# Projecting batch 1's queries with tokens on partitions, and a remainder matmul over all 128 rows

## The chip, the cores and the metric

The kernel runs on one core of one Trainium2 chip. The metric is the time of one execution in microseconds (us), as the device measures it; the median of several runs counts. The profile is one execution recorded by the hardware profiler. TensorE (PE in the profile, its weight loads PEld) multiplies matrices, VectorE (DVE), ScalarE (ACT) and GpSimd (POOL) do elementwise work, and SyncE (SP) issues the transfers.

## The reference

Linear attention followed by a two-layer MLP. For batch b and head h:

```python
def phi(x):
    proj = np.einsum('bhsd,df->bhsf', x, w_phi)
    proj = proj - np.max(np.abs(proj), axis=-1, keepdims=True)
    return np.concatenate([np.exp(proj), np.exp(-proj)], axis=-1)
q_p, k_p = (phi(q), phi(k))
kv = np.einsum('bhsf,bhsd->bhfd', k_p, v)
z = np.sum(k_p, axis=2)
num = np.einsum('bhsf,bhfd->bhsd', q_p, kv)
den = np.einsum('bhsf,bhf->bhs', q_p, z)[..., None] + 1e-06
x = num / den          # 4608 tokens x 512 after the heads are joined
h = x @ w_in           # 512 -> 2048
out = np.maximum(0.01 * h, h) @ w_out   # 2048 -> 512
```

There are 8 batches of 8 heads, 576 tokens and 64 channels; phi has 128 features of each sign. Everything is float32.

## The kernel before, in words

**Precision.** Most products are formed from two rounded parts each. A value x is split into a high part (rounded to the format fp32r) and the remainder, and a product is the sum of high x high, high x low and low x high: three fp32r matmuls. Some attention matmuls of the first batches are plain float32 ones instead; the trace has two records for each.

**Attention** works on pairs of heads; phase number i stands for pair i % 4 of batch i // 4. A k phase projects a pair's keys, exponentiates, and sums features against values into an accumulator (tile `c`); a q phase projects the queries, exponentiates, multiplies with what the k phase left and divides. Batch 0 (i = 0 to 3) has its own functions and runs first. From i = 4 on, `attention()` runs k phase i and q phase i - 1 in turns: both are generators, and each `yield` hands over to the other.

**Two forms of the query projection.** In `q_phase` (L301, all pairs from i = 4) the features stand on partitions and tokens in the free dimension: two matmuls for each of two heads and two half rows of 288 tokens (L319, L320), 32x32 block transposes on VectorE (L321, L340), a maximum over features that needs a reduction (L323) and six small steps across partitions (L325 to L330), a subtraction (L338), the exponentials on ScalarE (L345, L346), the matmuls with the k phase's result (L360), copies of numerator and denominator (L367, L368), and a normalization of all 576 tokens at once (L371 to L376). In `first_q_phase` (L468, batch 0) tokens stand on partitions: three matmuls for 128 tokens and both heads (`proj`, L379), one reduction along the free dimension (L486), one subtraction (L488), transposes on TensorE (L494), exponentials of a whole group of 256 tokens, the matmuls (L516), and a normalization of each group by itself (L523 to L527).

**The last 64 tokens of the keys.** 576 is 4 x 128 + 64. In k phases from i = 8 on, the fifth chunk keeps its 64 tokens in partitions 64 to 127 of the key tile `kst`, and their remainders in partitions 0 to 63 (L269), so that one matmul with `vh` (the same 64 values in both halves) adds high x high and high x low together (L272). The value remainders `vl` of these tokens lie in partitions 64 to 127 alone, and their matmul takes those 64 rows (L271).

**The MoE** takes blocks of 256 tokens (18 blocks). `split` makes the two parts of a block's input x from the ring of attention outputs, head pair by head pair; `layer1` (L568 to L571) accumulates over the four pairs, `layer2` (L588 to L590) follows three steps later. Block 2 is tokens 512 to 767: 64 of batch 0 and the first 192 of batch 1. Block 4 is tokens 1024 to 1279, and is the first with tokens of batch 2. `load_weights` (L146 to L168) rebuilds the weights from two halves of the stored number and splits them, on VectorE and ScalarE; w0 is the first layer's weight and w1 the second's, h and l their parts.

**What sets the order.** A scheduler orders each engine's instructions by priority when the program is built: first batch 0's attention, then the later attention (priority L599), then the weights (L623), then the MoE (L625), each as far as the data that the scheduler expects allow. Each engine then runs its list strictly in order. The accumulators of attention rotate over three buffers of tile `a`.

Of the kernel before, what the change touches and what calls it, by code (L numbers as in the profile page):

```python
# [9 lines left out]
F32 = mybir.dt.float32  # L10
F32R = mybir.dt.float32r
# [33 lines left out]
def attention_moe_kernel(ctx: ExitStack, tc: tile.TileContext, q, k, v, vt, w_phi, w_in, w_out, out):  # L45
# [8 lines left out]
    def st(shape, dt, tag):  # L54
        return sp.tile(shape, dt, tag=tag, name=tag, bufs=BUFS.get(tag, 1))
# [40 lines left out]
    vh = ct([P, 10, 66], F32R, "vh")  # L96
    vl = ct([P, 10, 64], F32R, "vl")
    nc.gpsimd.memset(vh[:, :, 64:66].bitcast(F32), 1.0)

    fr1, fr4 = (cp.tile([P, 2048], F32R, tag="late", name=n, bufs=4) for n in ("fr1", "fr4"))  # L100
    f2, f3 = (cp.tile([P, 2048], F32, tag="late", name=n, bufs=4) for n in ("f2", "f3"))
# [87 lines left out]
    def k_phase(i):  # L189
# [24 lines left out]
        for g in range(3):  # L214
            w = 2 if g < 2 else 1
            r = slice(0, P) if g < 2 else slice(64, P)
            n = P if g < 2 else 64
            m4 = st([P, 4], F32, "m4")
            pmk = st([P, 4, F], F32, "pmk")
            if nat:  # L220
                pk = pt("a")
                for s in range(w):
                    t0 = (2 * g + s) * P if g < 2 else S - P
                    proj(pk, s, kh[:, t0 : t0 + P], kl[:, t0 : t0 + P])
                pkv = pk[r, 0 : 256 * w].rearrange("p (a f) -> p a f", f=F)
            else:
                for s in range(w):
                    t0 = (2 * g + s) * P if g < 2 else S - P
                    pk = pt("a")
                    for j in range(2):  # L230
                        nc.tensor.matmul(pk[:, 256 * j : 256 * j + 256], lhsT=ks[:, j, t0 : t0 + P],
                                         rhs=wq.rearrange("p a f -> p (a f)"), start=True, stop=True)
                    pk = pk[r].rearrange("p (j x f) -> p j x f", j=2, x=2)
                    x = pmk[r, 2 * s : 2 * s + 2]
                    copy_("pk", x, pk[:, :, 1])
                    nc.vector.tensor_tensor(x, pk[:, :, 0], x, op=ALU.add)
                    yield
                pkv = pmk[r, 0 : 2 * w]
            nc.vector.tensor_reduce(m4[r, 0 : 2 * w], pkv, axis=AX.X, op=ALU.max, apply_absolute_value=True)
            mb = m4[r, 0 : 2 * w].unsqueeze(2).broadcast_to([n, 2 * w, F])  # L240
            if nat:
                nc.vector.tensor_tensor(pmk[r, 0 : 2 * w], pkv, mb, op=ALU.subtract)
            else:
                tt_("ksub", pkv, pkv, mb, ALU.subtract)
            yield
            for s in range(w):
                c = 2 * g + s
                ek = st([P, 2, 256], F32, ("ek", "kph", "kpl")[c % 3] if nat else "ek")
                nc.scalar.activation(ek[r, :, 0:F], pmk[r, 2 * s : 2 * s + 2], AF.Exp)  # L249
                nc.scalar.activation(ek[r, :, F:256], pmk[r, 2 * s : 2 * s + 2], AF.Exp, scale=-1.0)  # L250
                if nat:
                    for j in range(2):
                        kv_mm(j, rv[r, 4 * j + c if c < 4 else 8 + j], ek[r, j], first=c == 0, last=c == 4)
                    yield
                    continue
                if c < 4:
                    kph = st([P, 2, 256], F32R, "kph")
                    kpl = st([P, 2, 256], F32R, "kpl")
                    copy_("kph", kph, ek)
                    tt_("kpl", kpl, ek, kph.bitcast(F32), ALU.subtract)  # L260
                    for j in range(2):
                        kv_mm(j, vh[:, 4 * j + c], kph[:, j], first=c == 0)
                        kv_mm(j, vl[:, 4 * j + c], kph[:, j])
                    for j in range(2):
                        kv_mm(j, vh[:, 4 * j + c], kpl[:, j])
                else:
                    kst = st([P, 2, 256], F32R, "kph")
                    copy_("kst", kst[r], ek[r])
                    nc.vector.tensor_tensor(kst[0:64], ek[r], kst[r].bitcast(F32), op=ALU.subtract)  # L269
                    for j in range(2):  # L270
                        kv_mm(j, vl[r, 8 + j], kst[r, j])  # L271
                        kv_mm(j, vh[:, 8 + j], kst[:, j], last=True)  # L272
                yield
        kvs = st([P, 2, 256], F32, "ek").rearrange("p a (b f) -> p a b f", b=2)[0:66]
# [23 lines left out]
    def blocks(x):  # L298
        return x.rearrange("p a b -> p (a b)").rearrange("p (c d) -> p c d", d=32)

    def q_phase(i):  # L301
        b, hp = divmod(i, NP)
        nat = i < NN
        rq = qraw.pop(i)
        qs = st([P, 2, S], F32R, "qs")
        for j in range(2):
# [24 lines left out]
        yield  # L331
        kvh, kvl = kvs_of[i]
        dn = tq[:, 0]
        if not nat:
            qhs = st([P, 2, 2, U], F32R, "qh")
        for j in range(2):
            tj = blocks(tq[:, j])
            nc.vector.tensor_tensor(tj, tj, m[:, j].unsqueeze(2).broadcast_to([P, 18, 32]), op=ALU.subtract)  # L338
# [4 lines left out]
            for u in range(2):  # L343
                eq = st([P, 2, U], F32, "eq")
                nc.scalar.activation(eq[:, 0], mb[:, u], AF.Exp)  # L345
                nc.scalar.activation(eq[:, 1], mb[:, u], AF.Exp, scale=-1.0)  # L346
                if nat:
                    es.append((eq, None))
                else:
                    qh = qhs[:, u]  # L350
                    ql = st([P, 2, U], F32R, "ql")
                    copy_("qh", qh, eq)
                    tt_("ql", ql, eq, qh.bitcast(F32), ALU.subtract)
                    es.append((qh, ql))
                yield
            for u in range(2):
                qh, ql = es[u]
                nm = pt("a")[:, 0:U]
                for t in range(2):
                    nc.tensor.matmul(nm, lhsT=kvh[:, j, t], rhs=qh[:, t], start=t == 0, stop=nat and t == 1)  # L360
                    if not nat:
                        nc.tensor.matmul(nm, lhsT=kvl[:, j, t], rhs=qh[:, t], start=False, stop=False)  # L362
                if not nat:
                    for t in range(2):
                        nc.tensor.matmul(nm, lhsT=kvh[:, j, t], rhs=ql[:, t], start=False, stop=t == 1)  # L365
                rr = slice(64 * j, 64 * j + 64)
                nc.scalar.copy(ring[rr, b % 2, hp, U * u : U * u + U], nm[0:64])  # L367
                nc.scalar.activation(dn[rr, u], nm[64:128], AF.Copy, bias=1e-6)  # L368
                yield
# [5 lines left out]
        x = ring[:, b % 2, hp]  # L375
        tt_("x", x, x, dt.rearrange("p a b -> p (a b)"), ALU.mult)  # L376
        yield

    def proj(pk, s, lh, ll, n=P):  # L379
        o = pk[0:n, 256 * s : 256 * s + 256]  # L380
        nc.tensor.matmul(o, lhsT=lh, rhs=bd_h, start=True, stop=False)
        nc.tensor.matmul(o, lhsT=lh, rhs=bd_l, start=False, stop=False)
        nc.tensor.matmul(o, lhsT=ll, rhs=bd_h, start=False, stop=True)

    def first_kvh(i):
        if i == 0:
# [150 lines left out]
    def attention():  # L537
        for i in range(NP, B * NP + 1):
            gens = [k_phase(i)] if i < B * NP else []
            if i > NP:  # L540
                gens.append(q_phase(i - 1))
            while gens:
                for it in list(gens):
                    if next(it, end) is end:
# [130 lines left out]
```

## Time and profile before

| | |
|---|---|
| three timed runs | 1243.72, 1244.25 and 1248.7 us, median 1244.25 |
| profiled execution, first to last instruction (the only time that the profile gives of it) | 1244.1 us |
| busy share of that span | TensorE 95%, weight loads 84%, VectorE 69%, ScalarE 65%, GpSimd 55% |
| mean granted TensorE clock | 0.986 |
| first matmul of blocks 0, 1, 2 and 4 | 65.9, 174.8, 238.9 and 387.0 us |

In the profile's rows a time is in us from the start of the span unless it is marked as a mean in ns; a group's row ends with the idle time of the engine just before its instructions. A busy time of TensorE counts overlapping matmuls; how much of the engine a matmul takes is seen from one start to the next. A row of windows gives a stretch, its length, the busy time and number of instructions of PE, PEld, DVE, ACT and POOL (those that have any), the granted clock, and the transfers' share and GB/s.

### The profile page before, as it was taken

The page shows a single profiled execution, that of the slowest core. Times are in us where ns is not written, and L with a number is a line of the kernel's source. Part 1 is how long each engine was busy: PE and PEld are TensorE (multiplying, and loading weights), DVE is VectorE, ACT ScalarE, POOL GpSimd, SP SyncE. Part 2 cuts the span into 40 slices and gives each one's busy share as a digit, 9 for nine tenths or more (in the row PEclk, how much of TensorE's full clock was granted, in tenths as well). Part 3 has the DMA queues.
Part 4 walks back from the last instruction along what each step waited for, and adds up shares of the span by engine and source line. Part 5 has one row for each costly group of instructions (what it writes and reads, how often), then busy time and mean ns, then how long its engine had stood idle before and what let it go on. Part 6 is the DMA issues. An engine that isn't in the chain of part 4 may idle for free. (4 is left out here: it accounts for less than half of the span.)

```text
span 1244.1 us, 21315 instructions
## 1 busy us (share of the span) xinstructions
PE 1183.8 (95%) x7554; PEld 1041.1 (84%) x7554; DVE 862.9 (69%) x1373; ACT 806.0 (65%) x2044; POOL 688.4 (55%) x711
## 2 busy tenths in 40 slices
PE   6889889989999999999999999999999999999998
PEld 5577568879888888899888988889988888999997
DVE  7999985688888888888888888816887788200000
ACT  6897766767677777777676777635766767433232
POOL 2132122466777776767667676835666766433232
PEclk9899989979999999999999999999999999999999
DMA  6544511011111111111111111100111100000000
GB/s 190 150 118 145 142 56 42 19 47 30 48 31 39 39 30 48 31 47 31 34 30 42 30 48 30 31 29 27 31 47 31 27 21 1 18 18 1 18 18 17
DMA packets 62777, 57.00 MB, mean 46 GB/s; under 512 B 45136, under 2 KB 46288, under 8 KB 62672
## 3 DMA queue, kind: packets, MB, share of 16 engines
q1 hardware_dynamic: 62672, 55.65, 15.7%
q8 instruction: 59, 0.97, 0.3%
q14 instruction: 46, 0.38, 0.1%
HBM read 46.20 MB, written 9.44 MB: 45 GB/s over the span
## 5 line engine op out<-in xcount | busy, mean ns | idle before, releaser
L72 POOL TENSOR_TENSOR gl<-g,gh 128x256 fp32r<-128x256 f32 x288 | 246.7, 860 | 300.7 <-ACT gh L67 239.9
L568 PE MATMUL h<-xh,w0h 128*128 128x256 f32 x1152 | 297.6, 285 | 6.0 <-ACT w0h L67 3.3
L569 PE MATMUL h<-xh,w0l 128*128 128x256 f32 x1152 | 296.7, 284 | 1.7 <-DVE w0l L72 1.6
L588 PE MATMUL acc<-w1h,gh 128*128 128x512 f32 x576 | 229.4, 399 | 7.7 <-DVE o L69 3.6
L568 PEld LDWEIGHTS h<-xh,w0h 128*128 128x128 f32 x1152 | 219.4, 190 | 18.4 <-ACT w0h L67 3.9
L569 PEld LDWEIGHTS h<-xh,w0l 128*128 128x128 f32 x1152 | 219.7, 191 | 13.6 <-DVE w0l L72 4.1
L589 PE MATMUL acc<-w1l,gh 128*128 128x512 f32 x576 | 227.9, 396 | 0.3 <-DVE w1l L72 0.3
L590 PE MATMUL acc<-w1h,gl 128*128 128x512 f32 x576 | 219.5, 396 | 0.3 <-POOL gl L72 0.3
L571 PE MATMUL h<-xl,w0h 128*128 128x256 f32 x1152 | 207.5, 284 | 0.9 <-POOL rv L179 0.5
L575 ACT ACTIVATE g<-h 128x256 f32<-128x256 f32 x288 | 108.6, 382 | 125.3 <-PE h L571 86.6
L72 POOL TENSOR_TENSOR ql<-eq,qh 128x576 fp32r<-128x576 f32 x96 | 158.1, 1657 | 34.3 <-DVE qh L69 23.6
L571 PEld LDWEIGHTS h<-xl,w0h 128*128 128x128 f32 x1152 | 167.9, 190 | 3.8 <-POOL rv L179 0.8
L67 ACT CAST gh<-g 128x256 fp32r<-128x256 f32 x288 | 115.0, 403 | 78.8 <-PE acc L589 77.5
L72 POOL TENSOR_TENSOR kpl<-ek,kph 128x512 fp32r<-128x512 f32 x72 | 103.4, 1436 | 50.3 <-PE c L211 26.9
L588 PEld LDWEIGHTS acc<-w1h,gh 128*128 128x128 f32 x576 | 108.4, 188 | 23.1 <-DVE o L69 4.8
L590 PEld LDWEIGHTS acc<-w1h,gl 128*128 128x128 f32 x576 | 106.5, 189 | 18.9 <-POOL gl L72 0.5
L589 PEld LDWEIGHTS acc<-w1l,gh 128*128 128x128 f32 x576 | 108.9, 189 | 14.0 <-DVE w1l L72 0.7
L69 DVE CAST qh<-eq 128x576 fp32r<-128x576 f32 x96 | 92.9, 969 | 38.2 <-ACT eq L346 28.0
L69 DVE COPY o<-acc 128x512 f32<-128x512 f32 x17 | 11.6, 682 | 129.1 <-DMA out_dram<-o 129.0
L345 ACT ACTIVATE eq<-mb 128x288 f32<-128x288 f32 x112 | 49.2, 439 | 73.0 <-DVE mb L340 63.9
L249 ACT ACTIVATE ek<-pmk 128x256 f32<-128x256 f32 (+1 forms) x128 | 53.3, 417 | 58.0 <-POOL pmk L72 19.2
L201 DVE TENSOR_TENSOR ks<-rk,ks 64x576 fp32r<-64x576 f32 x48 | 74.8, 1558 | 12.9 <-ACT ks L67 11.6
(208 smaller groups left out, 2471.4 us busy)
## 6 DMA issues: line engine op xcount, KB each, us to landing
out_dram<-o SPq DMA_DIRECT2D x35, 256.0 KB, 2.0
rk<-in_k_dram SPq DMA_DIRECT2D x30, 288.0 KB, 2.8
ring<-in_w_in_dram SPq DMA_DIRECT2D x16, 512.0 KB, 3.6
qh<-in_w_out_dram SPq DMA_DIRECT2D x16, 512.0 KB, 3.6
rq<-in_q_dram SPq DMA_DIRECT2D x28, 288.0 KB, 2.8
rv<-in_v_dram SPq DMA_DIRECT2D x30, 256.0 KB, 3.4
rv<-in_vt_dram SPq DMA_DIRECT2D x60, 32.0 KB, 3.0
f<-in_k_dram SPq DMA_DIRECT2D x2, 288.0 KB, 4.3
```

The source lines that it names most:

```text
L67: nc.scalar.copy(o, i)
L69: (nc.vector if e == "v" else nc.gpsimd).tensor_copy(o, i)
L72: (nc.vector if pick(key) == "v" else nc.gpsimd).tensor_tensor(o, a, b, op=op)
L201: nc.vector.tensor_tensor(ks[n, j], rk[o], ks[o, j].bitcast(F32), op=ALU.subtract)
L249: nc.scalar.activation(ek[r, :, 0:F], pmk[r, 2 * s : 2 * s + 2], AF.Exp)
L568: nc.tensor.matmul(ph, lhsT=weight(0, "h", ft)[:, d * P : d * P + P], rhs=xh[:, d], start=d == 0, stop=False)
L569: nc.tensor.matmul(ph, lhsT=weight(0, "l", ft)[:, d * P : d * P + P], rhs=xh[:, d], start=False, stop=False)
L571: nc.tensor.matmul(ph, lhsT=weight(0, "h", ft)[:, d * P : d * P + P], rhs=xl[:, d], start=False, stop=d == NP - 1)
L575: nc.scalar.activation(g, ph, AF.Prelu, alpha=0.01)
L588: nc.tensor.matmul(a, lhsT=gh[:, ts], rhs=weight(1, "h", ft), start=ft == 0, stop=False)
L589: nc.tensor.matmul(a, lhsT=gh[:, ts], rhs=weight(1, "l", ft), start=False, stop=False)
L590: nc.tensor.matmul(a, lhsT=gl[:, ts], rhs=weight(1, "h", ft), start=False, stop=ft == NFT - 1)
```

## The change

Pairs 4 to 7 (batch 1) get a q phase of the other form: `token_q_phase` splits the queries (the remainder on GpSimd, `tt_("qr", ...)`, where `q_phase` has two VectorE steps) and runs three groups of 256, 256 and 64 tokens (`units`) through `q_group`, whose steps are those of `first_q_phase`. Each group is normalized and written to the ring by itself. `q_phase` loses its branches for these pairs and is otherwise the same for pairs 8 to 31. The value remainders' matmul of the last 64 tokens takes all 128 rows: rows 0 to 63 of those columns of `vl` are set to zero once, at the start.

```diff
+    nc.gpsimd.memset(vl[0:64, 8:10].bitcast(F32), 0.0)
...
-                        kv_mm(j, vl[r, 8 + j], kst[r, j])
+                        kv_mm(j, vl[:, 8 + j], kst[:, j])
                         kv_mm(j, vh[:, 8 + j], kst[:, j], last=True)
...
+    def q_group(qh, ql, t0, w, kvh, x, pm, dn):
+        pq = pt("a")
+        ns = max(w // P, 1)
+        n = min(w, P)
+        for s in range(ns):
+            c = slice(t0 + s * P, t0 + s * P + n)
+            proj(pq, s, qh[:, c], ql[:, c], n)
+        m4 = st([P, 4], F32, "m4")
+        pqv = pq[0:n, 0 : 256 * ns].rearrange("p (a f) -> p a f", f=F)
+        nc.vector.tensor_reduce(m4[0:n, 0 : 2 * ns], pqv, axis=AX.X, op=ALU.max, apply_absolute_value=True)
+        nc.vector.tensor_tensor(pm[0:n, 0 : 2 * ns], pqv,
+                                m4[0:n, 0 : 2 * ns].unsqueeze(2).broadcast_to([n, 2 * ns, F]), op=ALU.subtract)
+        yield
+        tr = pt("a")[:, 0 : 2 * w].rearrange("p (j t) -> p j t", j=2)
+        for s in range(ns):
+            for j in range(2):
+                nc.tensor.transpose(tr[:, j, s * P : s * P + n], pm[0:n, 2 * s + j], ident[0:n, 0:n])
...
+        nc.scalar.activation(ee[0], tr, AF.Exp)
+        nc.scalar.activation(ee[1], tr, AF.Exp, scale=-1.0)
+        yield
+        nm = pt("a")[:, 0 : 2 * w].rearrange("p (j t) -> p j t", j=2)
+        for j in range(2):
+            for t in range(2):
+                nc.tensor.matmul(nm[:, j], lhsT=kvh[:, j, t], rhs=ee[t][:, j], start=t == 0, stop=t == 1)
+            rr = slice(64 * j, 64 * j + 64)
+            nc.scalar.copy(x[rr], nm[0:64, j])
+            nc.scalar.activation(dn[rr], nm[64:128, j], AF.Copy, bias=1e-6)
+        yield
+        dt = st([P, U], F32, "mb")[:, 0:w]
+        nc.vector.transpose(dt, dn)
...
+        tt_("x", x, x, dt, ALU.mult)
+        yield
...
+    def token_q_phase(i):
...
+        copy_("qx", qh, rq)
+        tt_("qr", ql, rq, qh.bitcast(F32), ALU.subtract)
...
+        for g, (t0, w) in enumerate(units):
+            yield from q_group(qh, ql, t0, w, kvs_of[i][0], ring[:, b % 2, hp, t0 : t0 + w],
+                               tq[:, g % 2, 0:DM].rearrange("p (a f) -> p a f", f=F), st([P, U], F32, "dn")[:, 0:w])
...
-                gens.append(q_phase(i - 1))
+                gens.append((token_q_phase if i - 1 < NN else q_phase)(i - 1))
```

The scheduler's order changes with it. Below, line numbers of the changed kernel differ from those of the kernel before: its L615, L616 and L618 are the first layer (L568, L569, L571), L212 is L211, L232 is L231, L304 to L306 are `proj`, L324 is the transpose and L333 the numerator matmul of `q_group`, L317, L318 and L339 to L342 its VectorE steps, and L415, L416, L418, L378 and L379 are `q_phase`'s matmuls (L360, L362, L365, L319, L320).

VectorE at the last part of the weights (`w1l` of the last w_out piece), before:

```order
L72 TENSOR_TENSOR w0l_992<-ql,w0h_991 128x512
L164 ISA ql<-ql,kvl 128x1024
L242 TENSOR_TENSOR pmk<-a,m_1421 64x256
L325 COPY ms<-m 64x36
L326 TENSOR_TENSOR m<-m,ms 64x36
L327 COPY ms<-m 32x36
L328 TENSOR_TENSOR m<-m,ms 32x36
L72 TENSOR_TENSOR w1l_1005<-ql,w1h_1004 128x512
L329 COPY m<-m 32x36
```

and now:

```order
L72 TENSOR_TENSOR w0l_993<-ql,w0h_992 128x512
L341 RECIPROCAL rc<-mb 128x8
L240 TENSOR_REDUCE m_1376<-a 128x4
L165 ISA ql<-ql,kvl 128x1024
L342 STREAM_TRANSPOSE mb<-rc 128x256
L243 TENSOR_TENSOR pmk<-a,m_1376 128x512
L317 TENSOR_REDUCE m_1396<-a 128x4
L72 TENSOR_TENSOR w1l_1006<-ql,w1h_1005 128x512
L318 TENSOR_TENSOR tq<-a,m_1396 128x512
```

Before, all of pair 4, pair 5 up to its steps across partitions, and the query split of pair 6 stand ahead of the last weight part. Now two groups of pair 4 stand ahead of it, the reduction and subtraction of its third, and one reduction of pair 5 (`m_1396`).

GpSimd where block 2's input is made (the product that normalizes into `ring`, and the last remainder `xl` of the block), before:

```order
L72 TENSOR_TENSOR pmk<-pmk,m_1997 64x256
L72 TENSOR_TENSOR ring<-ring,mb 128x576
L72 TENSOR_TENSOR vl<-rv,vh 128x512
L72 TENSOR_TENSOR vl<-rv,vh 64x128
L72 TENSOR_TENSOR xl<-ring,xh 128x192
```

and now:

```order
L72 TENSOR_TENSOR ring<-ring,mb 128x64
L72 TENSOR_TENSOR gl<-g,gh 128x256 x2
L72 TENSOR_TENSOR kpl<-ek,kph 128x512 x2
L72 TENSOR_TENSOR ring<-ring,mb 128x256
L72 TENSOR_TENSOR xl<-ring,xh 128x192
```

The last remainder of block 2 now follows the product of the last pair's first 256 tokens, where it followed that of all 576. On TensorE the attention matmuls that stand between MoE matmuls there become 23 where they were 34.

TensorE at the start of block 4, now; these are the last rows of 48 matmuls of attention without a MoE matmul between them, and the first row of the MoE behind them:

```order
L379 MATMUL a<-qs,wq 128x288
L212 MATMUL c<-kpl,vh 66x256 x2
L232 MATMUL a<-wq,ks 128x256 x2
L212 MATMUL c<-kph,vh 66x256
L212 MATMUL c<-kph,vl 64x256
L212 MATMUL c<-kph,vh 66x256
L212 MATMUL c<-kph,vl 64x256
L212 MATMUL c<-kpl,vh 66x256 x2
L378 MATMUL a<-qs,wq 128x288
L379 MATMUL a<-qs,wq 128x288
L615 MATMUL h<-xh,w0h_716 128x256
```

At the same block before, attention and MoE matmuls alternate in short runs:

```order
L281 MATMUL c<-ident,ek 128x66 x4
L319 MATMUL a<-qs,wq 128x288
L320 MATMUL a<-qs,wq 128x288
L590 MATMUL acc<-w1h_1004,gl 128x512
L568 MATMUL h<-xh,w0h_715 128x256 x2
L569 MATMUL h<-xh,w0l_716 128x256
L231 MATMUL a<-wq,ks 128x256 x4
L571 MATMUL h<-xl,w0h_715 128x256 x2
```

What moved: attention now stands later against the MoE. Before, the result of k phase 12 is transposed (L281) ahead of block 4's first layer, now well behind it.

More of the change, by code (lines that the diff above doesn't have):

```diff
@@ L299, in blocks, with proj @@
         return x.rearrange("p a b -> p (a b)").rearrange("p (c d) -> p c d", d=32)
+    def proj(pk, s, lh, ll, n=P):
+        o = pk[0:n, 256 * s : 256 * s + 256]
+        nc.tensor.matmul(o, lhsT=lh, rhs=bd_h, start=True, stop=False)
+        nc.tensor.matmul(o, lhsT=lh, rhs=bd_l, start=False, stop=False)
+        nc.tensor.matmul(o, lhsT=ll, rhs=bd_h, start=False, stop=True)
+    def q_group(qh, ql, t0, w, kvh, x, pm, dn):
[15 more added lines that the diff above has]
+                nc.tensor.transpose(tr[:, j, s * P : s * P + n], pm[0:n, 2 * s + j], ident[0:n, 0:n])
+        ee = [st([P, 2, U], F32, "eq").rearrange("p a b -> p (a b)")[:, 0 : 2 * w].rearrange("p (j t) -> p j t", j=2)
+              for t in range(2)]
+        nc.scalar.activation(ee[0], tr, AF.Exp)
[11 more added lines that the diff above has]
+        nc.vector.transpose(dt, dn)
+        rc = st([P, 9], F32, "rc")[:, 0 : w // 32]
+        nc.vector.reciprocal(rc, dt.rearrange("p (a c) -> p a c", c=32)[:, :, 0])
+        nc.vector.transpose(dt.rearrange("p (a c) -> p a c", c=32), rc.unsqueeze(2).broadcast_to([P, w // 32, 32]))
+        tt_("x", x, x, dt, ALU.mult)
+        yield
@@ new lines, in token_q_phase @@
+    def token_q_phase(i):
+        b, hp = divmod(i, NP)
+        rq = qraw.pop(i)
+        qs = st([P, 2, S], F32R, "qs")
+        qh, ql = qs[:, 0], qs[:, 1]
+        copy_("qx", qh, rq)
+        tt_("qr", ql, rq, qh.bitcast(F32), ALU.subtract)
+        if i + 1 < B * NP:
+            load_q(i + 1)
+        yield
+        tq = st([P, 2, 2, U], F32, "tq").rearrange("p a b c -> p a (b c)")
+        for g, (t0, w) in enumerate(units):
+            yield from q_group(qh, ql, t0, w, kvs_of[i][0], ring[:, b % 2, hp, t0 : t0 + w],
+                               tq[:, g % 2, 0:DM].rearrange("p (a f) -> p a f", f=F), st([P, U], F32, "dn")[:, 0:w])
@@ L301, in q_phase @@
     def q_phase(i):
         b, hp = divmod(i, NP)
-        nat = i < NN
         rq = qraw.pop(i)
@@ L333, in q_phase @@
         dn = tq[:, 0]
-        if not nat:
-            qhs = st([P, 2, 2, U], F32R, "qh")
+        qhs = st([P, 2, 2, U], F32R, "qh")
         for j in range(2):
@@ L346, in q_phase @@
                 nc.scalar.activation(eq[:, 1], mb[:, u], AF.Exp, scale=-1.0)
[L347 to L354, printed above, removed]
+                qh = qhs[:, u]
+                ql = st([P, 2, U], F32R, "ql")
+                copy_("qh", qh, eq)
+                tt_("ql", ql, eq, qh.bitcast(F32), ALU.subtract)
+                es.append((qh, ql))
                 yield
@@ L359, in q_phase @@
                 for t in range(2):
[L360 to L365, printed above, removed]
+                    nc.tensor.matmul(nm, lhsT=kvh[:, j, t], rhs=qh[:, t], start=t == 0, stop=False)
+                    nc.tensor.matmul(nm, lhsT=kvl[:, j, t], rhs=qh[:, t], start=False, stop=False)
+                for t in range(2):
+                    nc.tensor.matmul(nm, lhsT=kvh[:, j, t], rhs=ql[:, t], start=False, stop=t == 1)
                 rr = slice(64 * j, 64 * j + 64)
@@ L377, in q_phase @@
         yield
[L379 to L383, printed above, removed]
     def first_kvh(i):
```

## The prediction

> **What bounds the kernel now.** I read the page's totals first, then the clock row, then the windows, then single matmuls.
>
> ```profile
> PE 1183.8 (95%) x7554; PEld 1041.1 (84%) x7554; DVE 862.9 (69%) x1373; ACT 806.0 (65%) x2044; POOL 688.4 (55%) x711
> PEclk9899989979999999999999999999999999999999
> ```
>
> TensorE is busy 95% of the span, and its granted clock has dips only in the first quarter. An average over unlike stages says little, so I cut the span where the work changes (us; busy time and count of PE, PEld, DVE, ACT, POOL; clock; DMA).
>
> ```profile
> 93.00:174.00 81.00, 68.21 (x351) 51.97 (x350) 75.80 (x135) 59.19 (x133) 15.58 (x18) 0.94 0.43 123
> 186.00:249.00 63.00, 63.00 (x382) 54.61 (x381) 34.66 (x64) 42.46 (x113) 23.76 (x30) 1.00 0.12 31
> 249.00:252.50 3.50, 1.47 (x10) 1.03 (x8) 2.20 (x4) 2.45 (x7) 0.61 (x1) 1.00 0.40 143
> 252.50:266.20 13.70, 12.11 (x49) 10.30 (x50) 13.24 (x26) 7.66 (x19) 7.71 (x8) 0.50 0.24 65
> 266.20:1050.00 783.80, 763.96 (x5081) 684.26 (x5080) 628.87 (x951) 545.89 (x1423) 540.84 (x521) 1.00 0.12 33
> 136.50:139.90 3.40, 3.40 (x12) 2.23 (x11) 3.31 (x8) 1.36 (x4) 0.00 (x0) 0.50 0.62 200
> 170.60:174.00 3.40, 3.40 (x12) 2.19 (x11) 3.31 (x7) 0.49 (x3) 0.00 (x0) 0.50 0.50 143
> ```
>
> Three regimes. Up to 174 VectorE is 94% busy (75.80 of 81.00), since it still builds the weights, and TensorE has lost 12.8 us idle plus half of three 3.4 us stretches at clock 0.50 (the first and the last are shown), together 17.9 us. From 186 to 249, and almost all of 266 to 1050 (19.8 us idle in 784), TensorE is the bound. Between them lies one stall, shown here with what ended it.
>
> ```profile
> PE h L568 <- ACT w0h L67: 3.3, 2, 2.3
> PE h L568 <- ACT dn L520: 2.0, 2, 1.6
> 250.18 0.50 PE L231 MATMUL a<-wq,ks 128*128 128x256 f32 x2 [0.21 <-ACT tq L368]
> 252.57 0.47 PE L211 MATMUL c<-kph,vl 64*64 64x256 f32 x1 [1.88 <-DVE kph L69]
> 258.11 0.56 PE L568 MATMUL h<-xh,w0h 128*128 128x256 f32 x1
> ```
>
> The first row is the largest wait between 93 and 186: first-layer matmuls wait for weights. The second stems from the token form itself, in batch 0, and is priced below. The others show that after 250 no MoE matmul is left that may run: block 2 (from 258.11) needs the last queries of batch 1. A gap of 1.88 us is followed by 13.7 us at clock 0.50. I price that stall at 2.0 us idle in the 249 window, 1.6 in the next, and 6.0 for the half clock (half of the 12.11 busy us): 9.6 us.
>
> The Trainium skill ("TensorE: Matmul & The Clock Gate", Part 1) has the clock halve after an idle window of about 3.4 us and return after as long a busy one; here TensorE was busy 1.47 us of the 3.50 before the drop, and the half clock lasted four such windows. By the Trainium skill's rule a short stall would cost its idle time alone, 3.6 us; I take the row.
>
> **The change part by part. First, the rows of the remainder matmul.** The 48 matmuls of the last 64 tokens' value remainders (two in each of 24 k phases) use 64 rows now.
>
> ```profile
> L211 PE MATMUL c<-kph,vl 128*64 128x256 f32 x192 | 49.5, 280 | 0.0
> L211 PE MATMUL c<-kph,vl 64*64 64x256 f32 x48 | 16.0, 333 | 2.3 <-DVE kph L69 2.3
> 382.47 0.29 PE L569 MATMUL h<-xh,w0l 128*128 128x256 f32 x1
> 382.59 0.28 PE L568 MATMUL h<-xh,w0h 128*128 128x256 f32 x1
> 382.80 0.33 PE L211 MATMUL c<-kph,vl 64*64 64x256 f32 x1
> 383.06 0.39 PE L569 MATMUL h<-xh,w0l 128*128 128x256 f32 x1
> 383.28 0.28 PE L568 MATMUL h<-xh,w0h 128*128 128x256 f32 x1
> 383.87 0.28 PE L211 MATMUL c<-kph,vh 128*66 128x256 f32 x1
> 384.08 0.33 PE L211 MATMUL c<-kph,vl 64*64 64x256 f32 x1
> 384.33 0.34 PE L211 MATMUL c<-kph,vh 128*66 128x256 f32 x1
> 384.51 0.40 PE L231 MATMUL a<-wq,ks 128*128 128x256 f32 x2
> ```
>
> Durations overlap, so I read start to start. Two full-height matmuls of 256 columns start 0.12 apart (382.47, 382.59). Around the 64-row one the steps are 0.21, 0.26, 0.22, in sum 0.69 instead of 0.35. For the second of the phase (383.87 to 384.51) they are 0.21, 0.25, 0.18, in sum 0.64. The surplus is 0.33 + 0.29 = 0.62 us a phase, times 24 = **14.9 us**. With 128 rows all steps should be 0.12, since the x192 group has just the new shape. The low end is the difference of the recorded durations, 48 x (333 - 280) ns = 2.5 us. I take 14.9, because the queue moves at the steps and TensorE is the bound there. The new matmul also waits for VectorE's key remainder, but the value matmul behind it waits for that today. The added clearing of 64 rows is one GpSimd memset at the start, off every chain.
>
> The Trainium skill ("TensorE: Matmul & The Clock Gate", "Why this matters for your kernels") says that a matmul over 32 rows takes the time of one over 128, and by it this edit would be worth nothing; the steps above contradict it.
>
> **Second, TensorE's bill for tokens on partitions.** For each of the four pairs of batch 1:
>
> ```profile
> 240.28 2.10 PE L360 MATMUL a<-eq,kvh 128*128 128x288 f32 x8
> 242.01 0.62 PE L231 MATMUL a<-wq,ks 128*128 128x256 f32 x2
> 242.46 0.28 PE L568 MATMUL h<-xh,w0h 128*128 128x256 f32 x1
> 105.42 1.00 PE L516 MATMUL c<-eq,tq 128*128 128x64 f32 x8
> 106.26 1.06 PE L516 MATMUL c<-eq,f 128*128 128x64 f32 x8
> 76.18 0.63 PE L494 MATMUL a<-ident,pmk 128*128 128x128 f32 x4 [1.81 <-DVE pmk L488]
> 76.64 1.03 PE L516 MATMUL c<-qs,tq 128*128 128x256 f32 x4
> ```
>
> Eight float32 records of 288 columns and the two L231 behind them take 2.18 us; less 0.24 for those two, 0.243 each, so 0.216 at 256 columns. At 64 columns it is 0.84 / 8 = 0.105. Four transposes take 0.46, or 0.11 each. Removed per pair: 8 projections of 288 columns (0.13 each by width, 1.06) and 16 records (3.89), in sum 4.95. Added: 15 projections at 0.12 (1.77), eight transposes (0.9) and two of half size (0.1), 16 records at 0.216 (3.46) and eight at 0.105 (0.84), in sum 7.1. That is 2.1 us more, four times 8.6 us. The tail's two transposes use 64 rows, which by the steps above may cost 0.3 more a pair: **+9.8 us** (8.6 to 9.8).
>
> The token form also adds a wait. Both heads' numerators share one accumulator, and the second head's two matmuls wait until ScalarE has copied the first head's (the wait on dn, at most 1.6 us in one case). Behind them on TensorE stands whatever is next, MoE matmuls included. Twelve groups at 1.0 us, the mean of that row's two waits, would make 12 us with no cover, and 0 with full cover. I take nothing, because in the order other matmuls stand between the heads in nearly every group.
>
> **Third, VectorE's relief.**
>
> ```profile
> 106.00:249.00 143.00, 1.42 (x12) 1.33 (x11) 29.43 (x43) 5.82 (x15) 0.96 0.26 74
> 106.00:249.00 143.00, 3.97 (x16) 0.96 0.26 74
> L309 DVE TENSOR_TENSOR qs<-rq,qs 64x576 fp32r<-64x576 f32 x56 | 48.1, 859 | 1.4
> L374 DVE STREAM_TRANSPOSE mb<-rc 128x576 f32<-128x576 f32 x28 | 20.9, 747 | 0.3
> L486 DVE TENSOR_REDUCE m<-a 128x4 f32<-128x512 f32 x5 | 3.4, 674 | 0.0
> L488 DVE TENSOR_TENSOR pmk<-a,m 128x512 f32<-128x512 f32 x3 | 2.0, 677 | 0.0
> L523 DVE STREAM_TRANSPOSE mb<-dn 128x256 f32<-128x256 f32 x9 | 3.9, 438 | 0.8 <-ACT dn L520 0.8
> L525 DVE RECIPROCAL rc<-mb 128x8 f32<-128x8 f32 x9 | 1.7, 192 | 0.0
> ```
>
> The first two rows are windows of the tiles tq and ms: 29.43 and 3.97 of VectorE over four pairs, 8.4 a pair. With two L309 (1.7), one L374 (0.75), and about 1.0 for L329, L330 and L373 (an estimate from the ms steps, 0.25 each), a pair costs 11.9. New: a group of 256 tokens takes 0.67 + 0.68 + 2 x 0.44 + 0.19 = 2.4, the group of 64 about 1.4 by size, so 6.2. By the order of VectorE, the work ahead of the last weight part was pair 4 (11.9), some 6.0 of pair 5 and 1.7 of pair 6. It will be two groups, a third begun, and one reduction, 6.3. That is 13.3 us less, in a stretch that VectorE fills to 94%. The most this can give back is those 13.3; the least is nothing, if the loads or ScalarE turn out to hold the weights. I take 8: with 13.3 us cut from 81 and two pairs' extra 4.9 us put on TensorE, TensorE would be nearly full itself. GpSimd gets the query remainder and three products for one, in a stretch where it is busy 15.58 of 81.
>
> **Fourth, the stall at block 2.** Block 2 takes the first 192 tokens of batch 1, and so waits for the first group of the last pair, not the whole pair. In the order the run of TensorE's attention instructions ahead of block 2 shrinks, but does not vanish. Between 0 and 9.6 us are won; I take 5.
>
> **Fifth, a stall that arrives.** Attention now stands later against the MoE in the order. At block 4, the first with batch 2, 48 attention matmuls follow each other where none did; last in that chain are the remainders of the last pair on GpSimd. The nearest price is the stall at block 2, 9.6 us; the bounds are 0 and 12. I take 8, as more chain is left at that point.
>
> Sum, from the profiled span of 1244.1 (0.15 below the median of the three times, 1244.25): 1244.1 - 14.9 + 9.8 - 8 - 5 + 8 = **1234.0 us**.
>
> **The rivals.**
>
> Everything recovers: the weights come 13.3 us sooner, block 2 stalls no more and block 4 not at all. 1244.1 - 14.9 + 9.8 - 13.3 - 9.6 = 1216. For it: the VectorE share. Against: the order at block 4.
>
> Attention's pace takes the saving: in 266 to 1050 VectorE is 80% busy, and rounds might be paced by its chain, so that TensorE turns two thirds of its 14.9 us into idle time: 1234 + 10 = 1244. Against: only 19.8 us idle there now.
>
> The height of the matmul does not matter, the surplus belonging to something that stays, such as the change of weights between 66 and 64 columns: 1234 + 14.9 = 1249. Against: the x192 group changes between 66 and 64 columns too, at 0.12 a step. The Trainium skill's sentence on 32 rows gives this case.
>
> Slower: attention falls behind and stays behind. If blocks 4 and 6 both stall at the full 9.6 us with the half clock, block 2 keeps its own, and the weights give back 4: 1244.1 - 14.9 + 9.8 - 4 + 19.2 = 1254. It decides once new stalls exceed what is won by 11 us or more. For it: the order at block 4, and the long half clock after a short gap. Against: attention has the higher priority and catches up.
>
> **How the numbers follow.** Forecast 62% (its own range 1226 to 1242), full recovery 18%, attention's pace 7%, height of no matter 5%, stalls 8%. A measurement tells about 0.5% from no change, so the bounds are 1238 and 1250.5. Faster: 0.50 of the forecast's 0.62, all 0.18, and 0.01 of the pace case, 0.69. Same: 0.12 + 0.05 + 0.03 + 0.01 = 0.21. Slower: 0.10. The range 1220 to 1248 leaves out most of the full recovery and of the stalls, about 19%.
>
> **What would show it.** The vl group with 128 rows at steps of 0.12 and TensorE idle still near 20 us between 266 and 1050 prove the first term; idle above 30 there refutes it. The last weight part before about 168 proves the third. A half clock missing or shorter near 250 proves the fourth; a new one near 390, where block 4 starts, the fifth. TensorE's four query phases costing more than 12 us extra, or the last weight part no earlier than 174, would make the prediction wrong.

## The result, and the profile after

The changed kernel takes **1254.1 us** (median of four, 1252.8 to 1257.3), the kernel before 1245.05 beside it: a ratio of 1.0072 (95% interval 1.0058 to 1.0087). It is 0.7% slower, where 1234 was forecast. Its profiled execution has a span of 1251.2 us, against 1244.1 before. The totals and the clock row of the page say nothing of that:

```profile
PE 1184.7 (95%) x7654; PEld 1045.7 (84%) x7654; DVE 840.5 (67%) x1349; ACT 804.3 (64%) x2048; POOL 691.0 (55%) x724
PEclk9999999999998999999999999999999999999999
```

TensorE's busy time is the same (1183.8 before), VectorE has 22.4 us less. So again windows, first of the kernel after, then three rows of the same cuts before (us; busy time and count of PE, PEld, DVE, ACT, POOL; clock; DMA):

```profile
93.00:174.00 81.00, 74.19 (x434) 61.34 (x433) 67.92 (x118) 61.61 (x143) 25.17 (x29) 0.96 0.42 122
249.00:266.20 17.20, 17.20 (x126) 16.18 (x125) 10.79 (x20) 11.14 (x30) 8.85 (x12) 1.00 0.10 33
266.20:400.00 133.80, 126.03 (x816) 111.85 (x815) 114.40 (x173) 93.89 (x246) 90.95 (x87) 0.97 0.13 37
400.00:1050.00 650.00, 622.89 (x4153) 557.94 (x4152) 514.61 (x785) 446.03 (x1163) 438.91 (x425) 1.00 0.12 33
```

```profile
249.00:266.20 17.20, 13.58 (x59) 11.34 (x58) 15.44 (x29) 10.11 (x26) 8.32 (x9) 0.60 0.27 81
266.20:400.00 133.80, 131.92 (x893) 119.64 (x893) 114.14 (x173) 96.49 (x252) 97.40 (x93) 1.00 0.13 34
400.00:1050.00 650.00, 632.04 (x4190) 564.62 (x4188) 514.73 (x779) 449.41 (x1172) 443.44 (x429) 1.00 0.12 33
```

Up to 266 the change gives what was hoped: TensorE is busier between 93 and 174 (74.19 against 68.21), and the stall at block 2 is gone (17.20 of 17.20 at full clock, where 13.58 at 0.60 stood). Then it turns: 7.8 us idle and a clock of 0.97 between 266 and 400, against 1.9 us and 1.00 before, and 27 us idle from 400 to 1050 against 18.

The two parts of the change do what they say. The remainder matmul now has 128 rows; after (first its group, the 192 that had this shape before and the 48, then single matmuls in a full stretch):

```profile
L212 PE MATMUL c<-kph,vl 128*64 128x256 f32 x240 | 62.6, 283 | 0.1
397.51 0.28 PE L212 MATMUL c<-kph,vl 128*64 128x256 f32 x1
397.63 0.28 PE L212 MATMUL c<-kph,vh 128*66 128x256 f32 x1
397.75 0.28 PE L212 MATMUL c<-kph,vl 128*64 128x256 f32 x1
397.86 0.28 PE L212 MATMUL c<-kph,vh 128*66 128x256 f32 x1
```

Of the 48 matmuls that had 64 rows, 45 now start 0.11 to 0.12 us before the next one, three 0.17. The last weight part on VectorE, in the kernel before and then in the kernel after (start, duration):

```profile
174.92 1.14 DVE L72 TENSOR_TENSOR w1l<-ql,w1h 128x512 fp32r<-128x512 f32 x1 [0.15 <-ACT w1h L67]
```

```profile
160.89 1.09 DVE L72 TENSOR_TENSOR w1l<-ql,w1h 128x512 fp32r<-128x512 f32 x1
```

It starts 14.0 us sooner, and block 1 with it (161.1 against 174.8).

Where the lead goes shows at block 4. The first matmul of a block is a poor mark there: the first pairs' input is there early and the last pair's late. I use the start of the **third tile of the first layer** (a tile is 12 matmuls over all four pairs), which no block reaches before all pairs of its batch are done. Against the kernel before it stands at: block 1 -13.1, block 2 -13.1, block 3 -18.9, **block 4 -0.8**, block 5 -1.2, **block 6 +9.1**, block 7 +10.0, block 10 +13.8, block 17 +7.3 us.

First-layer matmuls at the start of block 4 in the kernel after: the first one, the last one that needs only pairs 8 to 10, the first that needs pair 11, and the first of the third tile:

```profile
370.25 0.28 PE L615 MATMUL h<-xh,w0h 128*128 128x256 f32 x1
372.02 0.29 PE L616 MATMUL h<-xh,w0l 128*128 128x256 f32 x1
392.13 0.58 PE L615 MATMUL h<-xh,w0h 128*128 128x256 f32 x1 [0.28 <-ACT xh L67]
394.91 0.39 PE L615 MATMUL h<-xh,w0h 128*128 128x256 f32 x1
```

Windows of these 21 us and of the half clock that falls into them, after; then the same 21 us before:

```profile
371.00:392.00 21.00, 15.93 (x81) 12.24 (x79) 18.21 (x28) 13.10 (x34) 15.48 (x14) 0.87 0.17 53
386.40:393.20 6.80, 6.03 (x25) 5.20 (x25) 5.19 (x10) 3.42 (x9) 4.25 (x4) 0.50 0.16 43
```

```profile
371.00:392.00 21.00, 21.00 (x144) 19.05 (x143) 17.07 (x25) 16.82 (x48) 16.29 (x21) 1.00 0.06 16
```

The first two tiles (the accumulator `h` has two buffers) do three of their four pairs by 372.3 and then stand for 20 us, until pair 11, the last of batch 2, is there. In that time TensorE has attention's matmuls and twelve of the second layer, from 378.2 on attention's alone. It does 81 in the window instead of 144, while VectorE is busy 18.21 of 21. Priced as the prediction priced block 2, this stall costs 5.1 us idle and half of the 6.03 busy us at half clock, 8.1 us. Behind it the rounds of attention are slower. Between the transposes of k phases 12 and 16 lie 141.0 us after and 129.4 before. Of the difference of 11.6 us, 2.9 is MoE work (its matmuls from start to start) that now stands between these two marks; most of the rest is waits. What TensorE waited for in these rounds (total, times, longest), after, and then before:

```profile
PE a L378 <- DVE tq L380: 2.3, 3, 1.1
PE c L212 <- POOL kpl L72: 1.9, 1, 1.9
PE c L212 <- DVE kvl L295: 1.3, 2, 0.8
PE h L615 <- ACT xh L67: 1.0, 1, 1.0
```

```profile
PE c L211 <- DVE kpl L72: 1.2, 1, 1.2
PE h L568 <- ACT g L575: 0.4, 1, 0.4
```

No wait stands out (the largest rows are shown): after there are 15 in all, 9.6 us, before 5 with 2.5 us.

### The profile page after: what moved, and what is told of

The parts are those of the page before. It is cut to its first block, busy times and chain, and to the rows that moved or that the text cites. A ratio compares the mean times of both kernels' runs of the same rounds, so it can differ in the third digit from the quotient of the medians.

```text
span 1251.2 us, 21516 instructions
## 1 busy us (share of the span) xinstructions
PE 1184.7 (95%) x7654; PEld 1045.7 (84%) x7654; DVE 840.5 (67%) x1349; ACT 804.3 (64%) x2048; POOL 691.0 (55%) x724
## 5 line engine op out<-in xcount | busy, mean ns | idle before, releaser
L72 POOL TENSOR_TENSOR gl<-g,gh 128x256 fp32r<-128x256 f32 x288 | 242.4, 846 | 275.1 <-ACT gh L67 214.7
L615 PE MATMUL h<-xh,w0h 128*128 128x256 f32 x1152 | 295.2, 284 | 6.7 <-ACT dn L567 2.2
L616 PE MATMUL h<-xh,w0l 128*128 128x256 f32 x1152 | 293.5, 282 | 1.3 <-DVE w0l L72 1.3
L615 PEld LDWEIGHTS h<-xh,w0h 128*128 128x128 f32 x1152 | 217.9, 189 | 18.7 <-ACT dn L567 3.0
L616 PEld LDWEIGHTS h<-xh,w0l 128*128 128x128 f32 x1152 | 218.0, 189 | 11.5 <-DVE w0l L72 2.1
L618 PE MATMUL h<-xl,w0h 128*128 128x256 f32 x1152 | 201.7, 283 | 0.7 <-POOL xl L72 0.7
L72 POOL TENSOR_TENSOR ql<-eq,qh 128x576 fp32r<-128x576 f32 x96 | 153.0, 1601 | 71.8 <-DVE qh L69 59.8
L618 PEld LDWEIGHTS h<-xl,w0h 128*128 128x128 f32 x1152 | 164.7, 189 | 3.1 <-POOL xl L72 2.0
L635 PEld LDWEIGHTS acc<-w1h,gh 128*128 128x128 f32 x576 | 108.8, 189 | 16.7 <-DVE o L69 2.7
L69 DVE CAST qh<-eq 128x576 fp32r<-128x576 f32 x96 | 95.6, 1002 | 35.7 <-ACT eq L404 24.7
L403 ACT ACTIVATE eq<-mb 128x288 f32<-128x288 f32 x96 | 42.2, 439 | 81.6 <-DVE mb L398 77.9
L72 POOL TENSOR_TENSOR ring<-ring,mb 128x576 f32<-128x576 f32 (+2 forms) x45 | 52.1, 1158 | 66.7 <-DVE mb L573 18.3
```

Source lines behind the costliest of these rows:

```text
L69: (nc.vector if e == "v" else nc.gpsimd).tensor_copy(o, i)
L72: (nc.vector if pick(key) == "v" else nc.gpsimd).tensor_tensor(o, a, b, op=op)
L615: nc.tensor.matmul(ph, lhsT=weight(0, "h", ft)[:, d * P : d * P + P], rhs=xh[:, d], start=d == 0, stop=False)
L616: nc.tensor.matmul(ph, lhsT=weight(0, "l", ft)[:, d * P : d * P + P], rhs=xh[:, d], start=False, stop=False)
L618: nc.tensor.matmul(ph, lhsT=weight(0, "h", ft)[:, d * P : d * P + P], rhs=xl[:, d], start=False, stop=d == NP - 1)
L635: nc.tensor.matmul(a, lhsT=gh[:, ts], rhs=weight(1, "h", ft), start=ft == 0, stop=False)
```

## The experiments

One number needs a word ahead. TensorE's list is fixed before the run, so it can be said how much MoE work (its matmuls at their start-to-start steps) stands in it **ahead of the transposes of a k phase**. More MoE ahead means that attention stands later. In the kernel before it is 91 us ahead of k phase 8, 177 ahead of k phase 12 and 264 ahead of k phase 16; in the changed kernel 105, 188 and 278.

All runs in one table (times in us; block columns are the third first-layer tile; the last column lies between the transposes of k phases 12 and 24, twelve rounds of attention; these four come from one profile each):

| kernel | median | ratio to before, 95% | block 2 | block 4 | block 6 | k 12 to 24 |
|---|---|---|---|---|---|---|
| before | 1245.0 to 1245.7 | | 262.2 | 395.7 | 528.2 | 393.7 |
| changed | 1254.1 | 1.0058 to 1.0087 | 249.1 | 394.9 | 537.3 | 406.7 |
| rows_only | 1232.0 | 0.9870 to 0.9903 | 260.7 | 391.8 | 525.2 | 397.1 |
| token_only | 1243.6 | 0.9976 to 0.9995 | 247.6 | 395.3 | 531.7 | 389.3 |
| tok7 | 1232.6 | 0.9879 to 0.9909 | 250.8 | 394.1 | 523.3 | 389.9 |
| tok456 | 1238.6 | 0.9926 to 0.9956 | 261.2 | 398.3 | 530.9 | 388.1 |
| rev7 | 1237.4 | 0.9922 to 0.9961 | 260.3 | 396.3 | 534.0 | 388.6 |
| rev4 | 1250.4 | 1.0034 to 1.0063 | 246.8 | 392.4 | 534.6 | 406.7 |
| late_w | 1230.9 | 0.9852 to 0.9908 | 258.1 | 394.3 | 524.4 | 385.9 |
| rotkpl13 | 1238.5 | 0.9931 to 0.9970 | 249.4 | 394.7 | 530.9 | 381.4 |
| yield13 | 1240.4 | 0.9955 to 0.9984 | 250.1 | 396.4 | 538.3 | 386.6 |
| early_w | 1243.8 | 0.9973 to 0.9997 | 252.4 | 390.8 | 526.8 | 398.3 |
| tok7_rot | 1227.2 | 0.9836 to 0.9866 | 251.7 | 394.1 | 525.2 | 384.2 |
| late_w_rot | 1226.2 | 0.9829 to 0.9862 | 253.7 | 389.8 | 521.2 | 382.9 |

The last column also holds the MoE work that stands between its two marks: by start-to-start steps (0.119 us for 256 columns, 0.232 for 512) it is 260 us in the changed kernel and in rev4, 250 in rotkpl13, 267 in rows_only. Without it 147 us are left in the changed kernel and in rev4, and 126 to 132 in all twelve others. These two alone have slow rounds.

### The two parts apart

**rows_only**, against the kernel before:

```diff
+    nc.gpsimd.memset(vl[0:64, 8:10].bitcast(F32), 0.0)
-                        kv_mm(j, vl[r, 8 + j], kst[r, j])
+                        kv_mm(j, vl[:, 8 + j], kst[:, j])
```

> The kernel before with one edit alone: the last 64 tokens' value remainders multiplied over all 128 rows, and the clearing of those rows. Theory A (TensorE's own time is the bound between 266 and 1050 us, as the prediction had it): the 14.9 us of surplus steps are won, 1229 to 1233 us. Theory B (the chain of attention rounds sets the pace there, and TensorE time given back turns into small gaps): 1239 to 1246 us, though the matmul's steps become 0.12.

Measured: 1232.0, 13.7 us less. Theory A's number; B is out for this part. Its window from the stall's end on:

```profile
266.20:1050.00 783.80, 764.25 (x5163) 694.79 (x5163) 635.46 (x972) 551.05 (x1438) 548.63 (x529) 1.00 0.12 33
```

In the same 784 us 82 matmuls more are done than before (5081), and TensorE idles 19.6 us where it idled 19.8: the steps saved were TensorE's own, and nothing took them back.

**token_only**, against the changed kernel (the memset is left out too):

```diff
-                        kv_mm(j, vl[:, 8 + j], kst[:, j])
+                        kv_mm(j, vl[r, 8 + j], kst[r, j])
```

> The changed kernel with the matmul of the last 64 tokens' value remainders put back to 64 rows: the token form of batch 1's queries alone. Theory A (TensorE's time adds up): 14.9 us above the changed kernel, 1266 to 1270 us. Theory B (attention's pace): the saving was worth little in the changed kernel, 1253 to 1262 us.

Measured: 1243.6, 2.1 us below the kernel before (1245.7 beside it). Both theories missed, by 9 us and more. Apart, the parts give -13.7 and -2.1; together +9.1. So 25 us belong to neither part and arise when they meet. The last columns say where: token_only loses its lead at block 4 just as the changed kernel does (block 4 at 395.3), but its rounds from 12 to 24 take 389.3 us, not 406.7.

**tok7** and **tok456**, against the changed kernel (`q_phase` has its branch for these pairs back):

```diff
-                gens.append((token_q_phase if i - 1 < NN else q_phase)(i - 1))
+                gens.append((token_q_phase if i - 1 == 7 else q_phase)(i - 1))          # tok7
+                gens.append((token_q_phase if i - 1 in (4, 5, 6) else q_phase)(i - 1))  # tok456
```

> The changed kernel with the token form for the last pair of batch 1 alone; the other three pairs have the form of the kernel before. Block 2 then gets its input early but the weights are not relieved. Theory B1 (the loss comes from MoE work that may run earlier, at block 2 through the early release and before through earlier weights): the release alone gives part of the lag, k phase 12 about 5 us late instead of 13, 1243 to 1249 us. Theory B2 (the loss comes from the token phases' own length in attention's chain, pair by pair): a quarter of the loss, 1240 to 1246 us. Theory A: 1232 to 1238 us.

> The changed kernel with the token form for the first three pairs of batch 1 and the form of the kernel before for the last: the weights are relieved, block 2 gets its input late. Theory B1 (MoE work that may run earlier): the stall at block 2 is there again, larger than before since weights and block 1 come sooner, and the lag at k phase 12 is smaller than 13 us; 1246 to 1254 us. Theory B2 (the token phases' own length): three quarters of the loss, 1248 to 1252 us, with the lag at k phase 8 nearly as large as in the changed kernel (7.7 us). Theory A: 1238 to 1245 us.

Measured: 1232.6 and 1238.6. By the totals theory A. The times that B2 gave, a loss by the number of pairs in the token form, are missed by 7 us and more, and those of B1 by 10 us (tok7) and 7 us (tok456); B1 was right only on tok456's block 2 (261.2, the early release gone). Neither has slow rounds from 12 to 24.

### Early MoE work, or the token form itself?

**rev7** and **rev4** change no work, only the order of the three groups of one pair:

```diff
-        for g, (t0, w) in enumerate(units):
+        for g, (t0, w) in enumerate(units[::-1] if i == 7 else units):   # rev4: i == 4
```

> The changed kernel with one edit: the last pair of batch 1 (pair 7) runs its three groups of tokens in the opposite order (64, 256, 256), so that the tokens block 2 needs come last. Work and weights are those of the changed kernel; only the early release of block 2 is undone. In the order of TensorE's list the transposes of k phase 12 then stand behind 182 us of MoE work instead of 188, those of k phase 16 behind 268 instead of 278. Theory R (the loss comes from MoE work that the early release lets run ahead of attention): the stall at block 2 is back with up to 9.6 us, the rounds from k phase 12 to 24 take 388 to 394 us as in the token form for three pairs, instead of 407; 1236 to 1242 us. Theory T (the token form's own cost, in TensorE's time or attention's chain, together with the 128 rows): 1252 to 1262 us.

> The control for the run before: the same reversal of the groups, but for pair 4 (the first of batch 1), on which block 2 does not wait. TensorE's order against the MoE is that of the changed kernel from k phase 8 on (105, 188, 278 us of MoE ahead of k phases 8, 12, 16). Theory R: nothing changes, 1251 to 1257 us. Theory N (the changed kernel's loss is an accident of its order, which any small edit removes): 1234 to 1246 us.

Measured: 1237.4 and 1250.4. rev7 has all of the changed kernel's work and is 16.7 us faster, with block 2 later by 11.2 us. Theory T falls. The control is 0.6 below the range of theory R and keeps the changed kernel's slow rounds to the tenth (406.7): the last 6391 of its 7654 matmul records, from the first tiles of block 2 on, stand in the changed kernel's order. Not any small edit removes the loss.

**late_w** adds work, in the weights' helper:

```diff
                 nc.vector.tensor_scalar(w, w, TINY, HUGE, op0=ALU.max, op1=ALU.min)
+                for _ in range(2 if n >= 19 else 0):
+                    nc.vector.tensor_scalar(w, w, TINY, HUGE, op0=ALU.max, op1=ALU.min)
```

> The changed kernel with the clamp of the last 13 weight pieces done two more times (a repetition that changes no value), some 13 us of extra VectorE work among the weights: the relief of the weights is undone, and the token form, the 128 rows and the groups' early release stay. Theory R in its wider form (MoE work that runs early, whatever lets it, is what attention loses by): the transposes of k phases 12 and 16 stand behind 183 and 271 us of MoE, no run of attention alone is left at block 4; the weights come at 172 to 176 us as before, the stall at block 2 stays away, 1232 to 1240 us, faster than the changed kernel though work was added. Theory T: 1254 to 1266 us.

Measured: 1230.9, 23 us faster than the changed kernel and 1.1 below the range of theory R. The last weight part came later than expected, 7 us after that of the kernel before:

```profile
181.83 0.85 DVE L72 TENSOR_TENSOR w1l<-ql,w1h 128x512 fp32r<-128x512 f32 x1
```

Block 4 still has its third tile at 394.3. Weights that come 21 us later than in the changed kernel cost nothing at block 4 and gain 12.9 us at block 6.

**early_w** is the reverse, on the kernel before:

```diff
-                nc.vector.tensor_tensor(wi, wi, cr, op=ALU.add)
+                if n < 16:
+                    nc.vector.tensor_tensor(wi, wi, cr, op=ALU.add)
```

> The kernel before with the addition of the low half of the number left out for the weights from the seventeenth piece on (those weights lack their low bits; half a us of VectorE work per piece, some 8 us, is saved). Theory W (the weights' relief is worth what the prediction took, 8 us of 13, so some 5 of 8): block 1 starts 5 to 9 us sooner and that stays to the end, 1236 to 1241 us. Theory L (attention, which has not become sooner, sets the time at blocks 2 and 4, so MoE work that starts sooner only waits there): the lead is gone by block 4, 1242 to 1248 us.

Measured: 1243.8, 1.15 us less. The last weight part:

```profile
156.57 0.65 DVE L72 TENSOR_TENSOR w1l<-ql,w1h 128x512 fp32r<-128x512 f32 x1
```

This is 18.4 us sooner, more than the work left out. The lead at the third tiles melts: 9.8 us at block 2, 4.9 at block 4, 1.4 at block 6. Theory L: weights that come sooner, which the prediction counted on for 8 us, are worth about 1.

### Where behind block 4, and by what?

**rotkpl13** and **yield13**, against the changed kernel. TensorE's order in rotkpl13 is that of the changed kernel up to 419.7 us, behind k phase 12. In yield13 it is the same up to 386.1, within the run of attention at block 4; from there on neighbours change places, earlier than its expectation says:

```diff
+        if i == 13:
+            cnt["kpl"] += 1          # rotkpl13: in k_phase, at its start
...
         yield
+        if i == 13:
+            yield                    # yield13: behind the key split
         kvp = pt("c")
```

> The changed kernel with the turn of the key remainders (three of four on GpSimd, the fourth on VectorE) shifted by one from k phase 13 on; each engine keeps its number of instructions. The order is that of the changed kernel up to k phase 12, the 48 attention matmuls at block 4 included, and another one behind it: k phase 16 stands behind 271 us of MoE instead of 278. Theory R1 (what was lost at block 2 and block 4 is what costs, and stays lost): 1250 to 1257 us. Theory R2 (most is lost behind block 4, between k phases 12 and 24, by the order that the lag leaves there, 407 us where other kernels need 388 to 397): the rounds from 12 to 24 take under 396 us, 1236 to 1245 us, and k phase 12 comes as late as in the changed kernel (near 402 us).

> The changed kernel with one empty step more at the start of k phase 13 (the two phases that take turns are shifted by one turn in that round). No instruction is added, removed or given to another engine; the order up to k phase 12 is that of the changed kernel (188 us of MoE ahead of k phase 12, the run of attention at block 4 included), and another one behind it (237 us ahead of k phase 14 instead of 233, then 271 ahead of k phase 16 instead of 278). Theory O (the loss from k phase 12 to 24 belongs to the order that was built there, not to the engine that makes the key remainders): those rounds take 382 to 397 us instead of 407, 1236 to 1245 us. Theory E (shifting the turns of the engines is what helped in the run before): 404 to 410 us there, 1250 to 1257 us.

Measured: 1238.5 and 1240.4. Both have block 4 where the changed kernel has it (394.7 and 396.4), and both get 14 to 16 us back behind it. The same window of the changed kernel, of rotkpl13 and of yield13:

```profile
450.00:790.00 340.00, 320.84 (x2125) 284.85 (x2124) 278.51 (x423) 234.96 (x607) 229.63 (x221) 1.00 0.13 36
```

```profile
450.00:790.00 340.00, 327.53 (x2227) 298.96 (x2228) 289.98 (x454) 252.08 (x651) 244.91 (x234) 1.00 0.14 39
```

```profile
450.00:790.00 340.00, 328.86 (x2198) 298.55 (x2197) 287.88 (x443) 246.93 (x637) 240.71 (x229) 0.98 0.14 37
```

The changed kernel gets 2125 matmuls done there, the others 2227 and 2198, yield13 even with a half clock of 13.7 us at block 6 (its 0.98). All engines are less busy in the changed kernel: none is the bound, the engines wait for one another. yield13 moves no instruction to another engine, so it is the order (theory O), not who makes the key remainders. In the last column of the table both seem to gain more, 25 and 20 us; part of that is MoE work that no longer stands between the marks (10 and 5 us).

**tok7_rot** and **late_w_rot** put the edit of rotkpl13 on tok7 and on late_w.

> The kernel with the token form for pair 7 alone and the 128 rows, with the same shift of the key remainders' turns from k phase 13 on. Theory O: in an order that loses little (389.9 us from k phase 12 to 24) the shift is worth little, 385 to 392 us there, 1228 to 1235 us. Theory E: the shift by itself saves 15 us or more here too, 1214 to 1220 us.

> The changed kernel with the repeated clamps of the late weights and the shift of the key remainders' turns from k phase 13 on together. Both took their loss away from the changed kernel by themselves (1230.9 and 1238.5 us). Theory O: they mended the same thing, the order from k phase 12 on, so together they give little more than the better of them: 1226 to 1232 us. Theory E: the shift adds its 16 us: 1213 to 1218 us.

Measured: 1227.2 and 1226.2, so 5.4 and 4.7 us from the shift where the changed kernel got 15.6 from it. Theory O, though tok7_rot is 0.8 us below both of its ranges: where the rounds were not slow, there was little to mend. Both are faster than both kernels, by 1.5% than the kernel before. tok7_rot does it without idle work: the token form for one pair, the 128 rows, and a counter. That the token form has a share in this is not shown: rows_only alone takes 1232.0 and tok7 1232.6, and the shift was not tried on rows_only.

## Why the prediction was wrong, step by step

**First, the rows: right.** 14.9 us were said, 13.7 measured alone, at the steps and not at the durations (2.5). The Trainium skill ("TensorE: Matmul & The Clock Gate", "Why this matters for your kernels") has a matmul over few rows take the time of a full one; here 48 of 64 rows cost 13.7 us more than 48 of 128, and the measurement decides. The test that I named for it, idle time above 30 us between 266 and 1050, came out against it in the changed kernel (35 us) though the step was right: that idle time had another source.

**Second, TensorE's bill: right.** No run isolates it, but the traces let it be added up. From start to start and without idle time, the projections, transposes and numerator matmuls of the four pairs take 18.7 us before and 28.0 after, 9.3 more where 8.6 to 9.8 were said. The wait on dn was taken as nothing. Between 93 and 266 it is small:

```profile
PE a L333 <- ACT dn L336: 1.7, 2, 1.2
```

**Third, VectorE's relief: right as a duration, wrong as a gain.** 13.3 us less work were worked out; the last part came 14.0 us sooner, and VectorE's total fell by 22.4 us, 5.6 a pair, where 11.9 less 6.2 were said. But 8 us were entered as if they reached the end. early_w shows 18.4 us of lead becoming 1.15. TensorE has the time that was won at block 1, but blocks 2 and 4 begin when attention has finished a batch.

**Fourth, the stall at block 2: it went altogether** (third tile 13.1 us sooner, no half clock). Again the time did not last.

**Fifth, the stall at block 4: this is the step that failed.** It was entered at +8, with a bound of 12, as one stall by the price of block 2's, and with nothing behind it. As a stall it had the right size, 8.1 us by that price. Two other things were wrong. The lead that there is does not last beyond block 4: -18.9 us at block 3 became -0.8 there, so the third and fourth terms could not simply be added up with it. In all fourteen kernels block 4 lies between 389.8 and 398.3, though block 2 varies from 246.8 to 262.2. And I let lateness end there. Behind it the list has attention and MoE in another order, in which rounds 12 to 16 take 11.6 us more. This was no term of the sum; rotkpl13 and yield13, whose order is the changed kernel's up to 419.7 and 386.1 us, show it as 14 to 16 us.

The second of the two made the number wrong. With another order from there on, rotkpl13 and yield13 take 1238.5 and 1240.4 us, inside the forecast's own range of 1226 to 1242. That the sum comes so near there, though the time won before block 4 was not kept, is partly luck. The signs that were named for the third, fourth and fifth terms all came (the last weight part at 160.9, no half clock near 250, a new one at 386.4); they show that each effect is there, not that its time reaches the end.

By the third tiles, the changed kernel still stands 1.2 us better than before at block 5, with its attention 13 us late (k phase 12). Then the unforeseen order costs some 10 us up to block 6 and 15 up to block 10, where the kernel is 13.8 us behind. From there to block 17 it gets 6.5 back, and the span ends at +7.1. The saved rows are the likely reason: between these two blocks the kernels with 128 rows gain 4.9 to 10.7 us on the kernel before, and token_only and early_w, without them, 0.0 and 0.7.

**The rivals.** "Attention falls behind and stays behind" has the time (1254) and part of the mechanism, with 8%. What was said against it, that attention has the higher priority and catches up, fails: at k phase 12 it is 13.0 us late, at 16 24.6, at 24 26.0, and only at 31 6.6. That its sum gives the measured time is luck, as its terms did not occur: block 2 keeps no stall, and block 6 has no half clock in the changed kernel. "Attention's pace takes the saving" is refuted for the saved rows by rows_only, but it is what happens to the time won before block 4. "Height does not matter" is refuted.

**What stays open.** Why just this order is slow is not settled. The slow rounds have many small waits (15, the longest 1.9 us) in eleven places. MoE standing 278 us ahead of k phase 16 goes with the slow rounds in the changed kernel and in rev4, and 271 and 272 with fast ones in rotkpl13, yield13, tok7, late_w and token_only; that is a mark, not a cause shown. That MoE work brought forward makes attention late is shown by rev7 and late_w together with their control; that it does so by standing ahead of attention's matmuls in TensorE's one list is my reading of the order.

## What to carry to other kernels

Time won on an engine ahead of a point where it must wait for another chain is gone at that point; before adding up gains, find the next such point and ask when the other chain gets there, with the new order. Where a builder orders the lists, measure parts apart and together: two parts worth -13.7 and -2.1 us gave +9.1, and a neutral edit to the order gave 14 back. A matmul over part of the rows is to be priced by the starts of its neighbours, not by its own duration.

## What the hardware showed that I had not expected

The half clock comes in whole windows: 3.4, 6.8, 10.2 or 13.7 us, multiples of 3.41, in all profiles (but for the last of a run, which the end cuts). The Trainium skill ("TensorE: Matmul & The Clock Gate", Part 1) has a free-running window of 3413 ns, and the lengths agree. It also has one busy window bring the clock back, and the longest stretch agrees: in yield13 TensorE was busy 8.07 us of the first three windows and all of the fourth, and behind that one the full clock is back.

```profile
528.61:538.85 10.24, 8.07 (x32) 6.92 (x33) 9.92 (x21) 5.05 (x12) 4.27 (x5) 0.50 0.15 45
538.85:542.26 3.41, 3.41 (x18) 3.41 (x17) 3.27 (x5) 2.60 (x9) 2.67 (x3) 0.50 0.54 130
```

How much of a window must be busy is not shown: the half clock went on behind one with 3.23 of 3.41 us busy (kernel before, from 252.55) and ended behind one with 2.84 (early_w, from 237.2). So a short stall can cost more than its idle time; in yield13 13.7 us of half clock follow a window with TensorE busy 1.1 of 3.41 us.

An order's time repeats closely: rev4, another program with the same list from block 2 on, has 406.7 us for twelve rounds, as the changed kernel has.
